# A new issue table for an attention and gated-MLP kernel on one Trainium2 core

## The chip, the cores and the metric

The kernel runs on one core of a Trainium2 chip. The metric is the device time of one launch in microseconds, as the median of several runs. Matrix products run on TensorE (PE in the profile, its weight loads PEld), elementwise work on VectorE (DVE), ScalarE (ACT) and GpSimd (POOL). SyncE (SP) issues the loads and stores.

## The reference

Two parts run one after the other: a recurrent linear attention over 768 steps for 4 batches and 8 heads of width 48, and a gated MLP on its output.

```python
for t in range(S):
    cur = einsum('bhd,bhe->bhde', u[None] * kt, vt)
    y[:, :, t] = einsum('bhd,bhde->bhe', rt, state + cur)
    state = wt[:, :, :, None] * state + einsum('bhd,bhe->bhde', kt, vt)
...
h = maximum(x @ w_in, 0.0)              # x: 4 x 768 x 384, w_in: 384 x 1024
u, v = h[..., :512], h[..., 512:]
v_n = (v - mean(v)) / sqrt(var(v) + 1e-06)
v_s = einsum('ts,bsd->btd', w_spatial, v_n) + b_spatial[None, :, None]
return (u * v_s) @ w_out
```

## The kernel before

**Attention.** Each batch is cut into 6 chunks of 128 steps, so there are 24 slots. A slot loads its decays W, keys and queries kr and values v (and, from slot 6 on, N, from which the bonus term is made on VectorE and POOL). slot_prep multiplies neighbouring decays (W2p, L442), scans them into F and E (L449, L454) and scales the keys and queries (L446, L456, L460). slot_a (L525), slot_d (L616), slot_y and slot_inter (both L560) are the small matrix products. They use the array in 64-wide pieces; everything else on TensorE uses it at full width. slot_x copies the output y, transposes it (yt, L669) and splits it into a high and a low part (xT).

**MLP.** Every product is made of three matmuls of split operands, high by high, high by low, low by high (mm3, L686 to L688). hv_unit makes the v half of the first layer (ph, 512 wide), scale normalises it (vh, vl), g_unit makes the u half (pu) and the spatial product (pv), adds the bias (L792), multiplies by us (L794) and splits the result into gh and gl (L796, L797). out_unit is the last layer (po) and its store (ot). In the first stretch the weights are loaded and split too (e_, wi, wo, ws, L350 to L361 and L329 to L331). check_w loads the decays once more (Nw) to check their range, in the buffer that N also uses.

**Buffers.** N has one buffer, W, v and dg two, kr three, the small accumulators in PSUM (ph, pu, pv, po, yt, pt, pg) three among them.

**The order of the work.** Each step is an op with the engines that it may run on and their costs in us, 1930 in all, 624 of them on TensorE. The string PLAN has one word for each op, in the order in which the code creates them: a letter for the engine (T TensorE, V VectorE, A ScalarE, G POOL, S SyncE) and a start in hundredths of a microsecond, in base 36. plan (L199) reads the table and sorts the ops by start; issue writes the instructions in that order. An engine takes its instructions in that order, and each waits for what it needs by semaphores, so a start is never a time that the chip keeps: it fixes the order on each engine, the fillers, and nothing else. fill puts filler matmuls (py<-zk, L893) into gaps that the table has on TensorE before the op `last`:

```python
for o, w in zip(self.ops, words):
    o.on, o.start = w[0], int(w[1:], 36) / 100
    assert o.on in o.eng
return sorted(self.ops, key=lambda o: o.start)
...
if t < last.start and o.start - b > GAP:
    cold = max(0.0, min(o.start, COLD) - b)
    warm(max(0.0, cold - 0.1) / 0.43 + max(0.0, o.start - max(b, COLD) - 0.1) / 0.224)
t = max(t, o.start + o.eng["T"])
```

Of the kernel before, what the change touches and what calls it, by code (L numbers as in the profile page):

```python
# [37 lines left out]
V504 A5k2 V5o3 S4it V4wy V4zd V51f V55w A5mc V5rn T27w T29t T2e2 A2hs A2jk A2mh S5k S7s Sgo Vur Tyf Vlw Vwp  # L38
V1ca Vov Vwg V137 V13w Gzk G1f3 A1un A1ty Gfo V1d8 T1ke V1p8 A1fo T12s A1ax T1ov T1vv T1fr V1j8 A1kc V22l T1ym
A20y V23b T26n A28i T2bq A2ct T2j2 T2lj T2o5 A2t0 A2w8 A2wv Smc Sbd S1es V18w T1lv G1dh V1ml V1jy V1fd G1i1  # L40
V1iv V1nj G1o1 V1ya A29k A2a9 V24n T256 V2da A24j T1r9 A1sr T2c7 T2fz T23t V288 A2dv V302 T2ho A2ju V2ll T2ng
A2pa T2qv A2ry T2ts T2vp T2xm A305 A35x A36k A3bf G3xh V3lw G3x1 G3y9 G3z1 G3zt V40i V41z A457 V4cq A41g A43s
V45n A4aq A4e4 G4im S1do S1fw S224 V28y T2rc G22t G2di V2an V25z V27z V2f3 V2jw G2k5 V2o1 A343 A3aq V2x1 T39s
V3cs A388 T31e A32w T2zj T3jt T382 V3c1 A3e5 V3l0 T3l7 A3py V3s9 T3ur A3w1 T3yq A40e T44m T473 T490 A4cp A4fj
A4jd S1pg S210 S2j9 V2vd T3b9 V2uf V30t V37e V2yd V35u V39n V3ac G39w G3ed A3ut A3hs V3n7 T3i1 V3tl A3ng T3h5
A3in T3vf T41u T3ml V3rj G3ss V3ve T438 A46m V484 T4cs A4ft T4k1 A4l4 T4mp T4pa T4r7 A4ud A4w5 A4wt S2g8 S2lb
S3mk V3hf T3nz G3cr V3j3 V3k2 V3em G3l8 V3mu V3oj G3n3 G3u3 A4a1 V41h V3wv T40d V49f V40q T3qz A3sh T4ax T4dh
T3z7 V47c V4bz T4f7 A4h7 V4io T4ly A4n8 T4ot A4pw T4t4 T4v1 T4wy A4zh A51a A51x A54q V585 V55o G57g V58o V597
G59w V5av V5e0 A5hl V5l3 A5ei A5pt V5tc V5bf A5d2 V5fa T5nq S3rn A47o S4aj A4qy S4tt A56b S596 A5r8 T32a T33q
# [999 lines left out]
```

## Time and profile before

| | |
|---|---|
| time, median of 3 runs | 366.39 us (364.48 to 369.11) |
| span of the profiled execution | 363.9 us; its time outside the span is not recorded |
| TensorE busy | 355.2 us, 98% of the span |
| VectorE busy | 277.7 us, 76% |
| ScalarE busy | 211.4 us, 58% |
| POOL busy | 138.2 us, 38% |
| DMA | 47.81 MB, mean 131 GB/s |

The page counts an engine as busy while an instruction of it runs. Matmuls are pipelined: one starts before the one before has ended, so a TensorE that is busy all the time can still be fed at more or less than its full pace. Times in the trace are from the first instruction; times in the table are from the table's own zero, and the two are compared at landmarks, operations that can be found in both.

### The profile page before, as it was taken

The numbers are of one execution on the slowest core, as the hardware profiler recorded it, in microseconds if no ns is written. First come the engines' busy times: TensorE is split into PE (matmuls) and PEld (weight loads), VectorE is DVE, ScalarE is ACT, GpSimd is POOL, SyncE is SP. The second block draws the span as 40 slices with busy tenths as digits, with TensorE's granted clock in tenths as the row PEclk, the third lists the DMA queues.
The fourth block names the chain that finished last, engine by engine and source line by source line (L and its number), as shares of the span: only waits on it lengthen the run. The fifth ranks groups of instructions, "written<-read, shape, count | busy, mean of one in ns | idle before, by whom it ended". The sixth has DMA issues, their size and how long they took to land.

```text
span 363.9 us, 11371 instructions
## 1 busy us (share of the span) xinstructions
PE 355.2 (98%) x4666; PEld 328.1 (90%) x4666; DVE 277.7 (76%) x591; ACT 211.4 (58%) x585; POOL 138.2 (38%) x182
## 2 busy tenths in 40 slices
PE   7999899999999999999999999999999999999998
PEld 6887686799999889799999999999999998899997
DVE  7899996888798988987999865878996876234330
ACT  2468896994555657792554587762454757721212
POOL 3334343412551665523641748133223514013220
PEclk9899999999999999999999999999999999999999
DMA  7977636564165365841456444613462441000101
GB/s 219 292 237 217 191 87 182 188 193 156 45 192 147 102 193 161 216 127 52 117 148 192 130 123 149 193 45 112 118 188 60 137 139 46 0 23 0 38 31 69
DMA packets 21546, 47.81 MB, mean 131 GB/s; under 512 B 2545, under 2 KB 10354, under 8 KB 21490
## 3 DMA queue, kind: packets, MB, share of 16 engines
q1 hardware_dynamic: 21346, 46.85, 43.8%
q8 instruction: 37, 0.61, 0.7%
q14 instruction: 19, 0.16, 0.2%
q10 hardware_dynamic: 144, 0.20, 0.1%
HBM read 42.32 MB, written 4.72 MB: 129 GB/s over the span
## 4 chain that ended last, share of the span: by engine, by line
PE 84%; DVE 7%; ACT 5%; issue 2%; DMA 1%; POOL 0%; DVEq 0%; ACTq 0%
PE pv L686 9%; PE pv L688 9%; PE pv L687 9%; PE py L560 6%; PE po L686 5%; PE po L688 4%; PE po L687 4%; PE ph L686 4%; PE ph L688 4%; PE ph L687 4%; PE pu L686 4%; PE py L893 4%; PE pu L688 4%; PE pu L687 3%; PE paw L525 3%; PE paw L616 3%
## 5 line engine op out<-in xcount | busy, mean ns | idle before, releaser
L686 PE MATMUL pv<-ws,vh 128*128 128x384 f32 x192 | 65.7, 342 | 0.2 <-ACT us L783 0.2
L688 PE MATMUL pv<-ws,vl 128*128 128x384 f32 x192 | 64.4, 335 | 0.0
L687 PE MATMUL pv<-ws,vh 128*128 128x384 f32 x192 | 64.3, 335 | 0.0
L792 DVE TENSOR_TENSOR t<-pv,b_sb 128x384 f32<-128x384 f32 x32 | 17.6, 552 | 26.8 <-PE pv L688 26.7
L686 PEld LDWEIGHTS pv<-ws,vh 128*128 128x128 f32 x192 | 36.0, 188 | 1.4 <-ACT us L783 0.9
L796 ACT CAST gh<-t 128x384 fp32r<-128x384 f32 x32 | 15.9, 512 | 36.5 <-DVE t L794 25.1
L687 PEld LDWEIGHTS pv<-ws,vh 128*128 128x128 f32 x192 | 36.1, 188 | 0.0
L688 PEld LDWEIGHTS pv<-ws,vl 128*128 128x128 f32 x192 | 36.0, 188 | 0.0
L686 PE MATMUL pu<-xT,wi 128*128 128x384 f32 x96 | 34.2, 357 | 0.0
L686 PE MATMUL po<-wo,gh 128*128 128x384 f32 x96 | 32.8, 342 | 0.0
L688 PE MATMUL pu<-xT,wi 128*128 128x384 f32 x96 | 32.4, 338 | 0.1
L688 PE MATMUL po<-wo,gl 128*128 128x384 f32 x96 | 32.3, 336 | 0.0
L687 PE MATMUL po<-wo,gh 128*128 128x384 f32 x96 | 32.3, 336 | 0.0
L687 PE MATMUL pu<-xT,wi 128*128 128x384 f32 x96 | 32.2, 336 | 0.0
L686 PE MATMUL ph<-wi,xT 128*128 128x512 f32 x72 | 30.6, 425 | 1.0 <-DVE bv L491 0.7
L688 PE MATMUL ph<-wi,xT 128*128 128x512 f32 x72 | 28.4, 394 | 0.0
L687 PE MATMUL ph<-wi,xT 128*128 128x512 f32 x72 | 28.2, 392 | 0.0
L505 ACT ACTIVATE AS<-id,dgs 128x64 f32<-128x64 f32 x76 | 20.1, 336 | 5.9 <-DVE dgs L497 5.8
L460 POOL TENSOR_TENSOR kr<-kr,E 112x512 f32<-112x512 f32 x13 | 16.4, 1264 | 15.8 <-DVE kr L446 7.6
L456 POOL TENSOR_TENSOR kr<-kr,F 112x496 f32<-112x496 f32 x13 | 16.2, 1247 | 15.2 <-DVE kr L446 6.7
L446 POOL TENSOR_TENSOR kr<-kr,W 112x256 f32<-112x256 f32 x16 | 16.1, 1009 | 15.0 <-DVE dgs L497 5.1
L794 POOL TENSOR_TENSOR t<-t,us 128x384 f32<-128x384 f32 x9 | 9.6, 1068 | 31.1 <-DVE t L792 29.5
(199 smaller groups left out, 969.7 us busy)
## 6 DMA issues: line engine op xcount, KB each, us to landing
kr<-in_tr_dram SPq DMA_DIRECT2D x24, 448.0 KB, 4.8
N<-in_nat_dram SPq DMA_DIRECT2D x18, 384.0 KB, 3.5
Nw<-in_gt_dram SPq DMA_DIRECT2D x16, 384.0 KB, 3.4
W<-in_tr_dram SPq DMA_DIRECT2D x24, 225.8 KB, 3.3
v<-in_nat_dram SPq DMA_DIRECT2D x24, 192.0 KB, 3.9
out_dram<-ot SPq DMA_DIRECT2D x18, 192.0 KB, 3.3
wst<-in_w_spT_dram SPq DMA_DIRECT2D x12, 192.0 KB, 3.7
out_dram<-ot SPq DMA_DIRECT2D x10, 96.0 KB, 3.6
```

What stands on the lines that cost most here:

```text
L446: op({"G": 0.9, "V": dve(half)}, lambda e, n=n: e.tensor_tensor(two(kr()[:, n])[:, :, :, n], two(kr()[:, n])[:, :, :, n], w_()[:, :, :, 1 ...
L456: op({"V": 0.68, "G": 1.07}, lambda e: e.tensor_tensor(seg(kr()[:, 0])[:, :, :L2 - 1], seg(kr()[:, 0])[:, :, :L2 - 1], F()[:, :, 1:].unsqu ...
L460: op({"V": 0.69, "G": 1.1}, lambda e: e.tensor_tensor(seg(kr()[:, 1]), seg(kr()[:, 1]), E().unsqueeze(3).broadcast_to([R, SUB * G, L2, 2]) ...
L505: e.mul(As()[:, j, g, :], id64, dgs()[:, j, g:g + 1])
L525: nc.tensor.matmul(pa()[ks, j, g * L:(g + 1) * L], kr()[rs, 0, ts_], kr()[rs, 1, ts_], start=True, stop=True)
L560: nc.tensor.matmul(py()[row][L * a:L * (a + 1), D * n:D * (n + 1)], x, z, start=(a, row) not in started, stop=not left[0], skip_group_chec ...
L686: nc.tensor.matmul(ps, ah, bh, start=first, stop=False)
L687: nc.tensor.matmul(ps, ah, bl, start=False, stop=False)
L688: nc.tensor.matmul(ps, al, bh, start=False, stop=last)
L792: op({"V": dve(HT)}, lambda: nc.vector.tensor_tensor(t1(), pv()[:, :HT], b_sb[:, tsl], ALU.add), r=[(pv, 0), ("b", 0)], w=[(t1, 0)])
L796: op({"A": act(HT)}, lambda: nc.scalar.copy(gh(), t1()), r=[(t1, 0)], w=[(gh, 0)])
L893: nc.tensor.matmul(pw, zk, zk, start=False, stop=True, skip_group_check=True)
```

## The change

The diff replaces the table, and nothing else. The number of words is the same. 292 words name another engine than before (instructions on VectorE: 578 words before, 583 after; ScalarE 404 and 394; POOL 169 and 174; TensorE 624 and SyncE 155 in both), the rest another start. The first word of the table stands for a filler matmul, the last three for the range check (L919 to L923). Cut to its first and last lines:

```diff
--- before.py
+++ after.py
 PLAN = """
-T2s S4g Tgq Aji Ajc S4x5 S5kl S6o Apg Vrs Vt1 Vxn Azp G12f Spf A1ph V1tz V1wl V1zy A221 G24f Sa0 A134 V15y
-V178 V1al A1co V1kw S28 S3c S8w Vib Tkh Vbe Vk0 Vky Vcx Gf4 Vfy Vgm Vmu Goq A115 A14p Vcc Vzc Ts1 V11e Toz Ar1
-T13o T15x Tx1 V10n A15e V1ej T18f A19v V1h2 T1s5 A1vc T1xl A23h Suq A1we V21n V2bl V2g0 A2qc G2xa Sng A1mu
-V1r1 V1sa V1uw A2gd V2i8 S1h0 A2kw V2n4 V2pq V2sq A2us V345 S2v6 A3to G496 S238 A3gn V439 S25r A34s V38c S3xz
-A4i8 V4r1 S4c7 A5nh V5qb S4ux A5gg V5ms S2sw A5tl G5yv S5jh A5uq V61n S1i4 A2o6 V2rf S5v7 A67e V6i0 S4jx A5af
-V5hp S4y9 A5l7 V6jc S1je A2yj V31r V32u V363 A3d0 V5co S2i5 A3ju V3m4 V3q7 V4h2 A53l V5j1 S2qm A3m6 V4gb V4pq
...
-Anl5 To7a To8q Toei Tofy Toom Toq2 Vos4 Goty Aoww Gp8c Tnll Tnpx Tnrd Anwe Tpnb Tpor Tpw0 Tpxg Tq1s Tq38 Vq5a
-Vq70 Aq8p Gqae Tnn1 Tnoh Tnst Anvc Tq4o Tq64 Tq7k Tq90 Tqag Tqbw Vqdy Vqfl Aqhb Vqiv Toxb Toyr Tp5z Ap81 Tpq8
-Tpro Tpt4 Tpuk Tpyw Tq0c Vq2e Gq48 Aq76 Vq8q Tqho Tqj5 Tqm1 Tqnh Aqpj Sqr3 Tqdc Tqes Tqox Tqqd Aqsf Sqtz Tqg8
-Tqkl Tqrt Tqt9 Aqvb Sqwv Vn8u Tnlb Vp1v
+T2j S3j Tay Ad7 Ade S3oy S2on S5l Amk Voj Vqe Vse Axq Vzt Snc A1k8 V1ma V1qh V1t3 A1v4 G1y7 S9p A138 V15h V16q V1ac
+A1gz V26o S2i S4k S8o Vh2 Tj4 Vax Vj2 Vk0 Vc6 Ve6 Veq Vfe Vky Vmm Ax2 Az7 V78 Vxk Tow Vu2 Tn2 Apq Tz9 T12f Tx1 V12s
+A14u V1c0 T17r A19n V1cr T1eg A1fx T1he A1ig S1ao A2ar V2ep V2iz V2lm A2q1 V2ta Sod A1q3 V1s6 V1us V23b A25c V2hb S25b
+A2ir V2kp V2na V2qo A2ve V2xs S3jg A40k G430 S15d A32n V3ol S4ch A4tr V4xq S2po A46i V4na S3yl A4uw V4wf S4gl A58z
+V5cd S4ej A50e V51w S4ox A5i9 G5lb S2f5 A45d V4bs S57i A5xp G627 S58j A5jz G64u S4y2 A5el G5nz S2d2 A388 V3ae V3ca
+V3ho A4bd V50c S2nm A3ar V4d3 V4ek V4g7 A4z9 V54h S2e3 V4b2 V4du V4hi V4l8 A52m V582 S47l V4ki V4mk V4z1 V55s A57t
...
+Soyy Tmfv Tmhb Tmir Amks To37 To4n To63 To7j To8z Toaf Vocg Voe2 Aofq Gohd Tmk7 Tmln Tmvs Amxs Toup Tow5 Toxl Tp4t
+Tp6a Tp7q Vp9q Vpdy Api1 Gpjv Tn30 Tn4g Toow Aoqx Tpc2 Tpdi Tpey Tpge Tphu Tpja Vplb Vpmy Apol Vpq3 Tnxe To0b To1r
+Ao3r Toz1 Tp0h Tp1x Tp3d Tp96 Tpam Vpcm Vpf9 Apgw Vpie Tpm7 Tprz Tptf Tpxr Apzs Sq17 Tpkq Tpnn Tpuv Tpwb Apyc Spzr
+Tpp3 Tpqj Tpz8 Tq0o Aq2o Sq43 Vm4p Tq24 Vq2z
 """
 
 GAP, FILL_TO, COLD = 0.3, 5, 7.0
```

Where the prediction gives a planned start, it is such a word: the first ph of the old table is `T27w`, 28.76 us, its first pv starts at 70.54 and its last po at 347.49 us; the new table's at 337.20 us, with the range check's matmul (L921, at 305.75 us in the old table) behind it at 337.72. The op `last`, up to which gaps get fillers, stands at 73.34 us in the old table and at 141.85 in the new one.

## Rows read from the trace of the kernel before

**Rows 1.** The page: span, and busy time of the engines.
```profile
span 363.9 us, 11371 instructions
...
PE 355.2 (98%) x4666; PEld 328.1 (90%) x4666; DVE 277.7 (76%) x591; ACT 211.4 (58%) x585; POOL 138.2 (38%) x182
```

**Rows 2.** Busy time by stretch: stretch, length, then PE, PEld, DVE, ACT, POOL, clock, DMA.
```profile
0.00:28.00 28.00, 24.99 (x346) 22.20 (x346) 24.26 (x53) 12.93 (x33) 9.90 (x23) 0.94 0.87 252
28.00:75.00 47.00, 43.59 (x703) 35.48 (x703) 40.49 (x86) 39.85 (x109) 19.93 (x24) 1.00 0.59 173
75.00:360.00 285.00, 284.37 (x3602) 268.32 (x3601) 212.99 (x454) 158.11 (x444) 108.32 (x135) 1.00 0.39 113
```

**Rows 3.** What TensorE waited for, 28 to 75 us, then 75 on: us, times, longest.
```profile
PE paw L616 <- DVE S L631: 0.8, 1, 0.8
PE ph L686 <- DVE bv L491: 0.7, 1, 0.7
...
PE ph L686 <- DVE t L792: 0.3, 1, 0.3
PE pv L686 <- ACT us L783: 0.2, 1, 0.2
```

**Rows 4.** Busy time by stretch, 30 to 90 us, columns as in rows 2.
```profile
30.00:50.00 20.00, 18.96 (x285) 15.13 (x279) 19.52 (x38) 17.99 (x55) 9.56 (x8) 1.00 0.59 168
50.00:70.00 20.00, 18.48 (x362) 14.76 (x353) 15.83 (x37) 15.67 (x39) 9.42 (x16) 1.00 0.56 168
70.00:90.00 20.00, 20.00 (x174) 19.32 (x173) 16.84 (x39) 15.66 (x40) 4.03 (x7) 1.00 0.62 186
```

**Rows 5.** Instructions of ph, pv, po: count, ns (least/median/most), first and last start.
```profile
L686 PE MATMUL ph<-wi,xT x72: 387/397/684, 31.0 to 314.6; 128*128 128x512 f32 x72
...
L686 PE MATMUL pv<-ws,vh x192: 333/334/446, 78.0 to 353.1; 128*128 128x384 f32 x192
...
L686 PE MATMUL po<-wo,gh x96: 332/336/444, 95.4 to 359.3; 128*128 128x384 f32 x96
```

**Rows 6.** The timeline of TensorE, full-width matmuls: start, us, instruction.
```profile
352.58 0.33 PE L686 MATMUL pv<-ws,vh 128*128 128x384 f32 x1
...
353.10 0.33 PE L686 MATMUL pv<-ws,vh 128*128 128x384 f32 x1
```

**Rows 7.** The chain in order of time, one run of small matmuls: start, us, work.
```profile
215.40 1.08 PE py L560 x64
216.47 0.48 PE paw L525 x32
216.96 0.43 PE paw L616 x14
```

**Rows 8.** What VectorE waited for, 28 to 75 us.
```profile
DVE bv L491 <- PE py L560: 3.2, 1, 3.2
```

**Rows 9.** Lines on VectorE and POOL, columns as in rows 5.
```profile
L446 DVE TENSOR_TENSOR kr<-kr,W x32: 400/418/1385, 7.2 to 274.9; 112x256 f32<-112x256 f32 x32
...
L456 POOL TENSOR_TENSOR kr<-kr,F x13: 1038/1227/1847, 12.7 to 286.3; 112x496 f32<-112x496 f32 x13
```

**Rows 10.** Loads of N and kr: us to landing; who waited for N.
```profile
  POOL N L467: 1.6, 1
  DVE N L467: 0.7, 2
DMA to landing us min/median/max: 2.8/3.5/5.2
...
kr<-in_tr_dram SPq DMA_DIRECT2D x24, 448.0 KB, 4.8
```

**Rows 11.** The end: last store (KB, us to landing), and the loads of `bad`.
```profile
out_dram<-ot ACTq DMA_DIRECT2D x1, 192.0 KB, 1.9
...
L990 SPq TENSOR_LOAD <-bad x1: 479/479/479, 336.6 to 336.6; - x1
L990 PEldq TENSOR_LOAD <-bad x1: 742/742/742, 360.1 to 360.1; - x1
```

More of the change, by code (lines that the diff above doesn't have):

```diff
@@ new lines @@
+V2zt T3a1 V3ec A35q T36a A39j T3in T3m0 T3bd V3dm A3ew V3m6 T3na A3qd V3t8 T3wo V3y5 T427 A44a T47p T4az T4cv A4fd
+A4h5 A4in S2c1 S27d S39f V38q T3cs G340 V3b5 V3jj V36e G3gl V3j7 V3kh G3dr V3mw A3le A3ko V3qu T3pa V3uj G3qz T3kb
+A3m3 T3xc T3zc T3oj V3sh G3w7 T40m V42u V44i T471 V48i T4ai A4ci T4es T4go T4il A4l3 A4mv A4ni A4pj G4sb V4r8 G4rw
+G4sy V4tl V4u3 V4un V537 A56f V59d A5a4 A5cg V5e8 V4v5 A4wr V5fx Tay1 S3fr A3uu S3xk A48q S4bg A4q2 S4ss A53r T2w5
+T2xl T34u A3c2 T54x T59a T5aq T5f2 T5je T5kv V5pm V5u7 A5vu V67s T2z1 T30h T31y A33y T50l T56e T57u T5gi T5nr T5p7
@@ new lines @@
+V5r7 V5x5 A65q V6gi T33e T3f3 T3gj A3ij T5qo T5s3 T5uz T60s T654 T66k V6as V6dw A6fj G6ja T42o T444 T45l A47o T521
+T53h T5c6 T5dm T5hy T5mb V5ob G5qn A66w V6ck T6jr T6l7 T6tw T6vc A6xc S99e T6ib T6mn T6xg T6yw A74s S85w T6o3 T6pj
+T6r0 T6sg A6ug S6vv T4kh T4lx T4ou A4sp T5tj T5wf T63o T68w T6ff T6gv V6j4 V6u8 A6yf G702 T4nd T4qa T4t6 A4y6 T7js
+T7o5 T7pl T7r1 T7sh T7xi V7zi G81b A870 V88i T4rq T4um T4z5 A51k T7gw T7ic T7l9 T7mp T7tx T7vd V82r G84j A88v G8aj
+T5xv T5zc T628 A64o T70d T71t T739 T74p T765 T77l V7cu V7ky A7mm V7uc T8c7 T8dn T8f3 T8io A8ko Sa0d T8aq T8h7 T8k4
@@ new lines @@
+T8lk V8sc S8ty T9rk T9t0 T9ug T9vw A9xx S9zc S346 S3ao S56h S3nx G3um V3pw G3s9 V3wf V42m V445 V45t G45n V4iu V5hm
+V5jv V5lh A5dw G48h V5qy A5n4 A5yu A5rh A5zg T4xh V63n T49m A4hg V5t9 T6ao T4we V573 A5fr V5si T6by A6go V6lq T6ws
+V749 T791 A7cd T851 T86y T88u A8bc A8d4 A8dr S3kt S3zm S5n3 S4fk V4qb V5ix V5zs V4rj V57v V65g V664 V5vi V693 V5yg
+V60q V62c A6e6 A5wz A6av V6c3 A6ew A6bh G6oa T6dr V72g A626 T680 A69n T7aq T6co V6ni A6zk V75j T7ef A7iv V7ma T7wt
+A7ya T84k A85y T8n0 T8xt T8zq A928 A967 A96u S4di S4z2 S63y S6ev G6ax G6ly V6ta V6o8 V6rw V6yl V70r V6q8 G74i V6f7
@@ new lines @@
+V6ht V6kg A6vi A75u V6t2 V6n2 V6na V78w A723 T7c0 V7f8 A7df T79i A7b5 T80m T7dc V7ib V7rl V7so T82y A84w V8d5 T8gj
+V8i0 V8r1 T8u0 T8vx T91m A944 A95w A98r A9as G9g6 V9ef G9fr G9gt G9hg V9i5 V9kb A9mu A9p6 G9r4 Aa0e Aa7y Ga9w V9ym
+Aa6i Vb9p S611 S6du S6m2 S7cn G72x V77y V6s4 V76a G7cz V7e5 V7j2 V79v V7pw V6vn V6xa V6yx A7nr A886 V70j A7fy V7kq
+G7g7 G7o0 T7za V8vb A7zd T7g0 A7hn T93v T81w V8a2 A8vk V91w T96g V98d V9ar T9pf V9qw V9si Ta70 Ta8x Taat Aadq Aafo
+Aagb S6ww S7gc S70k S82j G7mf V8eg V7te V7o8 V89u V8as V8bg G8fv V8p4 V7bi G7di V7h1 A8fo G8d6 A8lq V8x4 V92n A8mc
@@ new lines @@
+G93n T954 V9fl G98b T8sp A8uc T9mk T97q V99t G9b0 V9he T9nu A9qm V9tt Ta09 Aa5g Vaaa Tade Tafb Tah7 Aajp Aalh Aam4
+S7hd S84x S7in S95s G8l4 G8is G8mq V8tn V8xc V8xw V8yk V909 G958 V7wr G7yj V81g V9kj A9yz A8p2 V8qt V9aj A9ub V9en
+T9kh V9zw V9jk T995 A9bc Ta45 T9lt V9v4 V9w6 Ta5f Va7d Va8y Tacq Vaek Vag6 Taj4 Tal0 Tamx Aapf Aat0 Aatn Aavo Vawz
+Vax5 Vaxo Gayd Vaz0 Vazi Vb01 Ab5q Abbj Vbhn Vb5i Ab9u Gbbr Vb0k Ab25 Vbfz S83k A8ge S8j4 A8y2 S90s A9cj S9f9 A9ro
+T9a1 T9q4 Ta0x Aa9e Tbey Tbkq Tbm7 Tbp2 Tbqj Tbrz Vc2a Gc48 Ac9q Gcgo T9bh T9cx T9ed A9ls Tc8m Tcaq Tcc6 Tcf2 Tcgi
@@ new lines @@
+Tchz Vcjz Vcs6 Acw0 Vczx T9ft T9h9 T9ip A9kq Tbge Tbhu Tbja Tbxr Tbz7 Tc0n Vc42 Vc6y Ac8l Vd4y T9xc T9ys Ta2d Aa4e
+Tb6z Tb8f Tbnm Tbtf Tbuv Tbwb Vbyc Gce0 Acgw Vd18 Tdcz Tdef Tdfw Tdhc Adjc Sdkr Tdjg Tdkw Tdmc Tdns Vdpt Shj3 Td77
+Td8n Tda4 Tdbj Addq Sdls Tapp Tav4 Tawk Ab7p Tcdm Tcjf Tckv Tcmb Tcp7 Td3u Vd9m Gdcx Adgq Vdiw Tayb Tb17 Tb2n Ab4n
+Tdp9 Tdqp Tds5 Te09 Te5a Te6q Veeb Geg3 Aej9 Vere Tazr Tb43 Tb5j Ab8s Teeo Teg4 Tele Tesj Tetz Texc Vf3f Vf7x Aff3
+Vfi2 Tcnr Tcx5 Tcyl Ad0m Tdtl Tdv1 Tdxd Tdyt Te2e Te3u Ve5u Ved0 Afdo Gffc Tfm4 Tfnk Tfrw Tftc Afvd Si9y Tgy9 Th21
@@ new lines @@
+Th3h Th4x Ah8l Sha0 Tfp0 Tfqg Tg1a Tg3f Vg8e Sga1 S8k5 S98e S9ue S9oh G922 G9l6 V9im V93w G99l V9c3 V9cr V9oj Va1p
+Va40 Ga5s Vabk Aasb A9zp Aaff Aadg Aad7 Gag7 Aaxf Tarh Vb2k Taot Aar3 Tba7 Tast Vb1t Gb31 Vb4j Tbct Abg0 Vbjk Tca2
+Vcbi Vcd4 Td01 Td1y Td5a Ad7s Adaj Ades S9af S9vf Sad6 Sa62 V9nl Gada Vam2 V9wy Ga01 Va3d Vacv Gahr Vap9 Vany Vasm
+Vau9 Vall Vavk Vbjc Vbco Abb9 Gbk1 Abda Tbbh Vbuq Vbf7 Tau8 Aaw8 Tc3b Tbdj Vbl3 Abm6 Vbzv Tc4l Ac6j Vcgg Tdis Adke
+Vdnw Tehk Tejh Teqn Aet5 Aeux Aevk S9pi Sa7c Savv Sbgr Vakn Vaw1 Van0 Vaqy Vb59 Vbse Vbt2 Gblm Gbz6 Vb6r Vb8e Vbbe
@@ new lines @@
+Abvd Vc3l Abh2 Abd1 Vbkv Abho Vboi Tc5u Vcla Ac0x Tc23 Ac3q Tcrv Tc76 Vcfq Aci2 Vcn3 Tcuh Ad9h Vdz4 Te1p Ae36 Ve84
+Temu Teor Tevf Aexx Aezp Af0c Af2d Vfba Vf98 Vf9s Vfbs Gfcg Gfd3 Gfdq Afp2 Ag2y Gg59 Afg9 Afil Gfv3 Vgjf Agvj Vh05
+Sanc Sbep Sbd0 Sc7j Gbv7 Gbsk Gbws Vc0l Gc2r Vcnu Vcoi Gcjc Vcqi Vbpg Vbr3 Vbwk Vd4g Adq1 Ac4y Vbzn Vc5e Gcm6 Vd3i
+Tct5 Vdm3 Acti Tcqn Acsa Te8i Tcvq Vd69 Gdg4 Ve0f Te9s Vebp Vevg Tf5i Af6z Vf9z Tg4v Tg6r Tg8o Agb6 Agfk Agg7 Sbfq
+Sc6i Sby5 Sd1d Vcth Vcyz Vd70 Vd7y Gdfl Vdgc Vdh0 Gda3 Gdm9 Gc8e Gcbb Vcef Gelu Vdr4 Ackk Adau Aekf Vd2k Vemp Teb1
```

112 lines of the change are left out of this document (34 added, 78 removed).

## The prediction

> **What bounds the kernel now.** I read the page's busy line first: TensorE is busy for 98% of the span, VectorE for 76%, and no other engine above 58% [rows 1]. A busy TensorE can be one that waits between pipelined matmuls or runs fillers, so the second view is busy time by stretch: TensorE is idle for 3.0 of the first 28 us, 3.4 of the next 47, and 0.6 of the last 285 [rows 2]. The third view, TensorE's own waits, says the same: from 28 to 75 us it waited for VectorE's sums (S) and products (bv), from 75 on for two things of 0.3 and 0.2 us [rows 3]. So the kernel has two regimes. Up to about 75 us TensorE waits for what VectorE prepares, which is itself nearly full: 19.5 of 20 us from 30 to 50 [rows 4]. After that TensorE alone sets the pace and a new order has almost nothing to take away.
>
> The fourth view is the trace laid beside the table. The table's words are planned starts, so each landmark of TensorE has a planned and a measured time. The first ph was planned at 28.8 and started at 31.0; the first pv 70.5 and 78.0; the last po 347.5 and 359.3 [rows 5]. The kernel thus runs 2.2 us late at the first ph, 7.5 at the first pv, 11.8 at the end.
>
> **The change part by part.** Nothing is added or removed: 1930 words before and after, 624 of them for TensorE. 292 words name another engine (POOL gets 5 instructions more, VectorE 5 more, ScalarE 10 fewer), all get another start. By the diff the last po moves from 347.5 to 337.2, so at face value the table promises 10.3 us. I don't take that at face value, because the old table charges TensorE for things that the new one prices lower: 64-wide operations at 0.5 where the new steps are 0.39 to 0.48, and idle slots of 0.20 before full-width work.
>
> *One price list for both.* Three 384-wide matmuls step on in 0.52 us: 352.58 to 353.10 [rows 6]. A run of four small-array operations takes 1.08 + 0.48 + 0.43 = 1.99 us [rows 7]; I book 0.46, 0.45, 0.48 and 0.39 for its four parts and 0.12 for each change of array width. With ph at 0.69 (its step in both tables) and the tables' other costs this makes 322.1 us of work ahead of the last po in the old order and 322.4 in the new one, which changes width 66 times against 62. What a landmark's time exceeds the work before it is TensorE's lost time.
>
> *Up to the first ph (11.4 us of work).* Old table 28.8, trace 31.0, new table 23.8 for the same work: it lets the first three slots' attention run ahead of the weight preparation, and emits 33 filler matmuls instead of 38. The trace's lateness of 2.2 us at this point I keep: VectorE was busy for 24.3 of the 28 us in front of it [rows 2], so there is no cover that would shrink it. 23.8 + 2.2 = 26.0, a gain of 5.0. Ends: a lateness of 0 (7.2 us won) and one of 7.2 (nothing won); I stay at what the row shows.
>
> *From there to the first pv (39.7 us of work).* The trace took 78.0 - 31.0 = 47.0, so 7.3 were lost. After the first pv 10.4 were lost over 526 operations and 20 small-array runs with hardly a wait; this stage has 75 operations and 6 runs, so about 2 of its 7.3 are the same hand-over cost that any order pays. The other 5.3 are waits. One is plain: VectorE once sat 3.2 us for TensorE (bv), and TensorE then waited for bv [rows 3, 8]. The new table has TensorE gapless from 25.7 to 112.6, so by its own count none remain. It buys this by filling VectorE: the idle time that the table leaves VectorE between 30 and 90 us falls from 10.7 to 4.6 us (starts, less the code's cost, less the 0.08 by which successive instructions overlap). VectorE instructions stretch when POOL reads at the same time: L446 takes 0.42 typically and 1.39 at worst, POOL's L456 1.04 to 1.85 [rows 9]. The table prices all of them at the short end. I take S = 4.5 us of waits, a little under the 5.3 of the trace, since the 3.2 us wait hung on the old order while the stretching stays. Ends: 0 (table) and 11.4 (second rival).
>
> By the Trainium skill, "SBUF — State Buffer", section "Who interferes with whom", a VectorE instruction with two SBUF inputs and a GpSimd instruction that reads SBUF exclude each other, and the later one blocks for the whole of the earlier. That speaks against this change: the time that the tables book for this pair from 30 to 90 us is 67.7 of 60 in the new one and 61.8 in the old, so by the rule alone 5.9 us more than before have to give way, S = 5.3 + 5.9 = 11.2 and 369.2 us, the second rival by another road. The trace agrees in part: the worst L446 lost 0.97 us, but the median, 0.418 against a least of 0.400, shows no block in most [rows 9].
>
> *From the first pv to the last po.* Trace 359.3 - 78.0 = 281.3 for 270.9 us of work, 10.4 lost, spread thin. I keep 10.4. The new order has 271.3 us of work here, and one hole that the old one had not: TensorE idles 1.5 us at 112.6 until the keys of slot 10 are ready (filled with five filler matmuls). 271.3 + 10.4 + 1.5 = 283.2. Bounds for the hole: 0, if TensorE is late there anyway, to 3, if VectorE is later still.
>
> *SP's queue and the DMAs.* Every load is moved with its step. Up to 130 us the old table has 5 loads whose first user stands within 4.1 us of the issue, the new one 16, mostly N, Nw and v. N lands 2.8 to 5.2 us after its issue, median 3.5; kr 4.8 [rows 10]. Behind a late N stand VectorE's whole queue (the product L467 is next in line) and, on SP, the kr and v loads. I put 0 on it in the sum, as ends 0 and 3.2 (11 more loads at about 0.3), because TensorE's work in this stretch lies 1 to 4 us behind its inputs in the new table.
>
> *The tail.* In the trace 363.9 - 359.3 = 4.6 us follow the start of the last po [rows 1, 5]: the last copy, its store, which lands 1.9 us after its issue [rows 11], and the end of the program. The new table moves the range check to the very end: its one-column matmul and the one-element comparison that writes `bad` now follow the last po, and only then can the five engines load `bad` (0.48 us on SP, 0.74 on TensorE) and branch [rows 11]. These lie beside the last copy and the 1.9 us of its store, so I count 0, with 0 and 0.7, one such load, as ends.
>
> *Sum.* 26.0 + 39.7 + 2.0 + S + 283.2 = 350.9 + S for the last po, against 359.3: a gain of 8.4 - S, with S = 4.5 a gain of 3.9. The profiled span becomes 360.0. The profile records no time of its own execution outside the span; the runs' median of 366.4 lies 2.5 above the span, the fastest run 0.6. I carry the gain over to the median: 362.5 us.
>
> **Rivals.** *The waits vanish too.* S = 0.4: 366.4 - 8.0 = 358.4 us. For it: TensorE has no gap in the table, and hand-overs are booked as short as the trace has them. Against: the old table was nearly as gapless here (2.1 us) and the trace lost 7.3.
>
> *VectorE and POOL slip: slower than before.* Place: 30 to 90 us. The old table's 10.7 us of VectorE slack took part of the stretching; the new one has 6.1 less. If all of that comes through to TensorE, S = 5.3 + 6.1 = 11.4, a loss of 3.0: 369.4 us. It decides from S = 8.4 on. For it: VectorE was busy 52.2 of these 60 us already [rows 4]. Against: from 70 us on TensorE was not tied to VectorE at all, 20.0 of 20 busy.
>
> *Loads just in time.* The 11 tighter loads cost their 3.2: S = 7.7, 365.7 us, no change. For it: the single N buffer makes these loads a serial chain. Against: in the whole trace POOL waited 1.6 us for N and VectorE 0.7 [rows 10].
>
> *The table keeps its word.* 10.3 us: 356.1. Against it stands the price list above.
>
> **How the numbers follow.** Forecast, S between 2.5 and 6.5: 0.48 (360.5 to 364.5). Waits vanish: 0.22. Just-in-time loads: 0.13. Slip: 0.14. Table's word: 0.03. The range leaves out the table's word, the better part of the first rival and the worst third of the slip: 357.5 to 369.0. A measurement of this kernel tells about 2% from no change, 7.3 us. Faster by more: the table's word and, of the first rival, the part with S under 1.1, together 0.15. Slower by more needs S above 15.7, the end of the slip: 0.04. Within: 0.81.
>
> **What would show it.** Right: first ph near 25 us and 11.4 us of work done by 26; first pv (51.1 us of work) near 72; TensorE idle under 1 us after 115 apart from the hole; last po near 356. The waits between 30 and 90 should name VectorE, its busy time there above 54 of 60 us. Wrong: TensorE idle at 110 to 120 of several us (slip), VectorE waits on N or v of more than 1 us in sum (loads), or a last po under 353 (no waits). If TensorE loses much less than 10 us after the first pv, the hand-over cost was not fixed, and the step that kept it was wrong.

## The result, and the profile after

The changed kernel takes 362.92 us (360.93 to 364.02, 9 runs) where the kernel before, on the same chip, takes 366.32 (364.48 to 369.11, 9 runs): a ratio of 0.9899, interval 0.9866 to 0.9932. The forecast was 362.5. In a second series (the last experiment) the same two kernels gave 360.60 and 366.20, ratio 0.9867 (0.9839 to 0.9894). So the change is worth 1.0 to 1.3%, real and below the 2% bound. The kernel before has medians of 365.9 to 366.3 us in all five series of this study, so ratios of different series can be compared.

The total came out as forecast. Its parts did not, so the hit is in good part luck. The page after, for [rows 1]:

```profile
span 361.1 us, 11353 instructions
...
PE 356.2 (99%) x4656; PEld 331.1 (92%) x4656; DVE 271.3 (75%) x596; ACT 211.1 (58%) x587; POOL 141.1 (39%) x187
```

Busy time by stretch after, for [rows 2] and then [rows 4], columns as there:

```profile
0.00:28.00 28.00, 25.35 (x289) 23.13 (x290) 22.41 (x49) 11.39 (x30) 9.21 (x21) 0.89 0.81 222
28.00:75.00 47.00, 46.87 (x814) 39.48 (x815) 44.10 (x97) 42.72 (x117) 19.37 (x27) 0.99 0.72 211
75.00:361.00 286.00, 284.02 (x3556) 268.46 (x3554) 204.80 (x451) 156.98 (x442) 112.54 (x140) 1.00 0.37 111
...
30.00:50.00 20.00, 20.00 (x332) 16.29 (x326) 19.05 (x38) 17.64 (x53) 8.20 (x10) 1.00 0.71 216
50.00:70.00 20.00, 19.87 (x382) 17.06 (x383) 18.48 (x44) 18.68 (x48) 10.14 (x14) 1.00 0.79 224
70.00:90.00 20.00, 20.00 (x173) 19.68 (x173) 18.76 (x44) 16.43 (x46) 5.03 (x7) 1.00 0.50 151
```

From 28 to 75 us TensorE is idle for 0.13 us where it was idle for 3.4. VectorE is busier: it works for 56.3 of the 60 us from 30 to 90, where it worked for 52.2 before, and TensorE hardly waits for it there. All of TensorE's waits of 0.2 us or more between 28 us and the last po, for [rows 3] (the 0.5 us stand at 196.6, the 0.2 at 91.1):

```profile
PE yt L665 <- DVE y L661: 0.5, 1, 0.5
...
PE pt L539 <- ACT us L779: 0.2, 1, 0.2
```

ph, pv and po after, for [rows 5] (the lines stand four lower in the changed kernel, so L686 is L682):

```profile
L682 PE MATMUL pv<-ws,vh x192: 331/334/446, 75.3 to 350.3; 128*128 128x384 f32 x192
...
L682 PE MATMUL po<-wo,gh x96: 332/336/445, 95.4 to 356.5; 128*128 128x384 f32 x96
...
L682 PE MATMUL ph<-wi,xT x72: 386/390/505, 30.7 to 308.4; 128*128 128x512 f32 x72
```

The first ph starts at 30.7, hardly sooner than the 31.0 of before; the forecast had it near 25. With the prediction's price list the trace splits into its three stages and the tail (us). "Again" is a second profile of the same changed kernel, an experiment below.

| | before | forecast | after | again |
|---|---|---|---|---|
| to 11.4 us of work | 31.0 | 26.0 | 31.3 | 28.3 |
| from there to 51.1 | 46.9 | 46.2 | 43.1 | 43.0 |
| from there to the last po | 281.4 | 283.2 | 282.1 | 282.3 |
| last po to the end | 4.6 | 4.6 | 4.6 | 4.6 |
| span | 363.9 | 360.0 | 361.1 | 358.2 |

The first stage gained nothing instead of 5.0 us, the second 3.8 instead of 0.7, the third lost 0.7 instead of 1.8. Errors of +5.3, -3.1 and -1.1 us leave 1.1 of span: the first two cancel by chance.

**Where the first stage lost its 5 us.** TensorE's first steps after; columns are start, us, engine, line, operation. L889 is the fillers, L415 slot 0's bonus (pg0), L521 slot 0's slot_a (sc0), L612 its slot_d (pd0); further down sc1 is slot 1's slot_a, and KT0 and yt0 are slot 0's transposed keys and output:

```profile
6.70 2.50 PE L889 MATMUL py<-zk 128*128 128x128 f32 x10
8.99 1.71 PE L415 MATMUL pg<-up_sb,rk 112*128 112x2 f32 x8
...
12.46 1.13 PE L521 MATMUL paw<-kr 48*64 48x64 f32 x32
13.53 3.32 PE L889 MATMUL py<-zk 128*128 128x128 f32 x20
16.78 0.67 PE L612 MATMUL paw<-v,KT 64*64 64x48 f32 x32
```

Two things are to be seen. pg0's operand rk0 was ready at 7.6 us, but ten filler matmuls, issued for a gap of the table, ran until 9.2. pd0's accumulators were free at 14.4, when VectorE's copy of sc0 (L525) ended, but twenty filler matmuls held TensorE until 16.8; the table had pd0 at 11.9. And the eight bonus matmuls take 1.71 us, which is 213 ns from start to start; at 2.4 GHz it is 112. TensorE ran at 1.2 GHz up to 15.3 us and again from 22.1 to 28.9. The granted clock by stretch (the last three columns are clock, DMA share, GB/s; ahead of the trace's first clock entry the column shows 1.00 whatever it was, and only the pace of equal matmuls tells):

```profile
0.00:15.29 15.29, 12.95 (x96) 12.37 (x97) 11.66 (x28) 4.51 (x10) 2.81 (x15) 1.00 0.86 219
15.29:22.11 6.82, 6.52 (x116) 5.64 (x116) 6.47 (x12) 2.61 (x7) 3.69 (x4) 1.00 0.90 267
22.11:28.94 6.83, 6.83 (x85) 6.07 (x85) 5.15 (x13) 5.16 (x15) 3.15 (x3) 0.50 0.49 151
28.94:75.00 46.06, 45.93 (x810) 38.55 (x810) 43.23 (x96) 41.83 (x115) 18.93 (x26) 1.00 0.74 216
```

That gives the theory for the first stage, called theory 1 below, which the experiments test: TensorE itself is late, by fillers and by its clock, and VectorE waits for it. For the second stage there are two candidates, the new order and the 292 new letters.

### The profile page after: what moved, and what is told of

It is laid out like the page before. It is cut to its first block, busy times and chain, and to the rows that moved or that the text cites. A ratio compares the mean times of both kernels' runs of the same rounds, so it can differ in the third digit from the quotient of the medians.

```text
span 361.1 us, 11353 instructions
## 1 busy us (share of the span) xinstructions
PE 356.2 (99%) x4656; PEld 331.1 (92%) x4656; DVE 271.3 (75%) x596; ACT 211.1 (58%) x587; POOL 141.1 (39%) x187
## 4 chain that ended last, share of the span: by engine, by line
PE 92%; DVE 4%; ACT 3%; issue 1%; POOL 0%; DVEq 0%
PE pv L682 9%; PE pv L684 8%; PE pv L683 8%; PE py L556 7%; PE ph L682 5%; PE ph L684 5%; PE pu L682 5%; PE ph L683 5%; PE py L889 4%; PE pu L684 4%; PE po L682 4%; PE pu L683 4%; PE po L684 4%; PE po L683 4%; PE paw L521 4%; PE paw L612 3%
## 5 line engine op out<-in xcount | busy, mean ns | idle before, releaser
L682 PE MATMUL pv<-ws,vh 128*128 128x384 f32 x192 | 65.6, 342 | 0.0
L682 PEld LDWEIGHTS pv<-ws,vh 128*128 128x128 f32 x192 | 36.1, 188 | 0.5
L682 PE MATMUL pu<-xT,wi 128*128 128x384 f32 x96 | 34.0, 354 | 0.1
L682 PE MATMUL po<-wo,gh 128*128 128x384 f32 x96 | 33.2, 346 | 0.0
L793 POOL TENSOR_TENSOR gl<-t,gh 128x384 fp32r<-128x384 f32 x14 | 14.7, 1053 | 44.4 <-ACT gh L792 44.2
L637 ACT ACTIVATE S<-S,prod 112x48 f32<-112x48 f32 x100 | 25.2, 323 | 9.3 <-DVE S L627 7.2
L711 ACT ACTIVATE hv<-ph 128x512 f32<-128x512 f32 x24 | 14.3, 594 | 27.7 <-PE ph L684 27.5
L682 PE MATMUL ph<-wi,xT 128*128 128x512 f32 x72 | 29.4, 409 | 0.0
L684 PE MATMUL ph<-wi,xT 128*128 128x512 f32 x72 | 28.3, 393 | 0.0
L683 PE MATMUL ph<-wi,xT 128*128 128x512 f32 x72 | 28.3, 392 | 0.0
L754 POOL TENSOR_TENSOR vl<-hv,vh 128x512 fp32r<-128x512 f32 x14 | 18.1, 1300 | 25.2 <-ACT vh L752 24.9
L779 ACT ACTIVATE us<-pu 128x384 f32<-128x384 f32 x32 | 15.1, 486 | 14.7 <-PE pu L684 14.6
```

The source lines that it names most:

```text
L637: e.mul(S1[i % 2][a][:, g, :], S0[:, g, :], Wc[:, g:g + 1])
L682: nc.tensor.matmul(ps, ah, bh, start=first, stop=False)
L683: nc.tensor.matmul(ps, ah, bl, start=False, stop=False)
L684: nc.tensor.matmul(ps, al, bh, start=False, stop=last)
L754: lambda e, hv=hv, vh=vh, vl=vl: e.tensor_tensor(vl(), hv(), vh().bitcast(F32), ALU.subtract),
L779: op({"A": act(HT, True)}, lambda: nc.scalar.activation(us(), pu()[:, :HT], AF.Relu), r=[(pu, 0)], w=[(us, 0)])
```

## The experiments

### No fillers ahead of pd0

```diff
-                if t < last.start and o.start - b > GAP:
+                if t < last.start and o.start - b > GAP and not 11 < o.start < 12:
```

> The changed kernel without the ten filler matmuls (20 records, 13.53 to 16.85 us) that stand in front of slot 0's decay product pd0, which started at 16.8 us though its input KT0 was ready at 12.65. Theory 1 (TensorE itself makes the first 30 us late, by fillers sized for the table's gap): pd0 starts at 12.7 to 13.5, 11.4 us of work are done by about 28 (31.3 in the changed kernel), time 359.5 to 361. Rival VectorE (the forecast's reason: VectorE is full here, 22.4 of 28 us): 11.4 us of work still done near 31, time 362.9. Rival clock (fillers are what lifts the granted clock): more of the stretch at 1.2 GHz, 11.4 us of work later than 32, time 363.5 to 365.

366.07 us, ratio 0.9984 (0.9954 to 1.0014), twelve runs from 363.4 to 369.1. Theory 1 by itself fails. The rival on the clock is nearest: the trace is at 1.2 GHz up to 27.8 us, and 11.4 us of work are done at 31.7. pd0 starts at 14.5, not at 13: it waits not for KT0 but for VectorE's copy of sc0, 13.7 to 14.4, which frees its accumulators, and sc0 was late already. What that wins is gone by sc1, at the slow clock. The profiled run was the longest of the twelve, so its end says nothing about the median; but it shows a loss of another kind, TensorE idle without a wait, in the middle of a row of 32 small matmuls:

```profile
59.60 0.58 PE L521 MATMUL paw<-kr 48*64 48x64 f32 x25 [1.74 <-issue]
```

### No fillers at all in the first 100 us

```diff
-                if t < last.start and o.start - b > GAP:
+                if 100 < t < last.start and o.start - b > GAP:
```

> The changed kernel without any filler in the first 100 us. Theory 1: 11.4 us of work done by 27 to 29, time 359 to 361. Rival VectorE: near 31, time 362.9. Rival clock: TensorE stays at 1.2 GHz up to 25 us or longer, real work there takes about twice its time, 11.4 us of work later than 32.5, time 364 to 366.

361.03 us, ratio 0.9854 (0.9818 to 0.9890): 1.9 us under the changed kernel's first series, level with its second one (360.60), so at least nothing is lost. 11.4 us of work are done at 29.3, 2.0 sooner than in the trace after, although TensorE is at 1.2 GHz up to 25 us at least: the bonus matmuls of slots 0, 1 and 2, the last from 20 us on, are all 213 ns apart, and the transposes pt at 25.4 us 204, where those at 39.0 are 97 apart. (From 27.6 us on the small matmuls run at their later pace, so it was not slow for the whole of the first 30 us.) Slot 0's steps in that trace, beside those of the changed kernel above:

```profile
7.76 1.84 PE L415 MATMUL pg<-up_sb,rk 112*128 112x2 f32 x8 [3.25 <-DVE rk L410]
...
10.37 1.13 PE L521 MATMUL paw<-kr 48*64 48x64 f32 x32
12.71 1.09 PE L612 MATMUL paw<-v,KT 64*64 64x48 f32 x32 [1.20 <-ACT vs L476]
```

pg0 now waits for VectorE's rk, 0.9 us behind the table, and pd0 is 0.8 behind where it was 4.9. By the first ph the lateness is back at 5.5. TensorE is busy for 11.96 of the 12 us from 16 to 28, at the slow clock, so the clock is the likely cause; no run without fillers has the fast clock beside it. The forecast's reason, a VectorE without cover, isn't it: VectorE gets more done in the same time here, 23.9 us busy of 28 against 22.4.

### More fillers from 12 to 24 us

```diff
-                b = max(t, free)
+                b = max(t, free); 12 < o.start < 23.6 and warm(1)
```

> The changed kernel with one filler more (two matmul records, some 0.33 us) in front of each TensorE step with a table start between 12 and 23.6 us. Rival clock: the stretch of granted clock 0.5 from 22.1 to 28.9 us goes or gets shorter, 11.4 us of work done by 29 to 30, time 360.5 to 362. Theory 1 (fillers stand in front of real work): 11.4 us of work later by 1 to 4, that is 32.5 to 35, time 364 to 367. Rival VectorE: TensorE's idle time takes the fillers up, no change, 362.9.

363.92 us, ratio 0.9973 (0.9935 to 1.0011), in two groups: seven runs from 363.1 to 364.1, five from 367.7 to 368.4. The profiled run, 367.7, has the granted clock down from 23.8 to 30.6 all the same and 11.4 us of work done at 36.3, 5.0 later. In that run fillers ahead of work cost more than theory 1's 1 to 4 us; what the faster group did is not in a trace.

### A long first gap, then almost none

```diff
-                    cold = max(0.0, min(o.start, COLD) - b)
-                    warm(max(0.0, cold - 0.1) / 0.43 + max(0.0, o.start - max(b, COLD) - 0.1) / 0.224)
+                    n = {394: 11, 1189: 3, 11401: 5}
+                    warm(n.get(round(100 * o.start), 0))
```

> The changed kernel with its early fillers laid out anew: 11 instead of 6 in the first gap (as many as the old table has there), 3 in front of pd0, none elsewhere in the first 100 us. Without any filler the first 30 us ran wholly at 1.2 GHz (eight bonus matmuls 213 ns apart, 112 at 2.4 GHz) and still 11.4 us of work were done 2 us sooner than in the changed kernel. Theory 1 (fillers in front of ready work cost, and the clock costs as well): the long first gap brings 2.4 GHz by 8 to 10 us at little cost, as in the run with the old head, 11.4 us of work done by 26.5 to 28, time 357.5 to 359.5. Rival: the later start of the spread matmuls (7 us instead of 3.4) delays everything behind it by as much as the clock gives, 11.4 us of work by 29.5 to 30, time 361. Rival: the clock falls again between 10 and 25 us, since TensorE idles there, 11.4 us of work by 29 or later, time 360.5 to 362.

365.98 us, ratio 0.9974 (0.9940 to 1.0008), 363.2 to 370.8. The last rival holds, and worse than stated: the clock is up at 5.7 us and falls at 9.1, at 19.3 and once more at 53.4. The second stage takes some 49 us, over 5 more than in the changed kernel: the second fall lasts into it, to 33.0, and the third lies in its middle. The stretches around it, and what TensorE did just before:

```profile
32.96:53.44 20.48, 19.39 (x340) 16.43 (x338) 18.53 (x39) 18.20 (x54) 8.43 (x9) 1.00 0.70 218
53.44:60.27 6.83, 6.83 (x46) 5.69 (x49) 5.30 (x14) 3.54 (x11) 3.65 (x6) 0.50 0.50 164
```

```profile
52.77 0.32 PE L612 MATMUL paw<-v,KT 64*64 64x48 f32 x7 [1.09 <-issue]
```

TensorE stood 1.09 us without a wait that the profile names, just ahead of the fall. In the changed kernel, 45.93 of 46.06 us busy after 28.9, the clock does not fall. But the stop alone is not shown to be the cause: the longer one without the ten fillers, 1.74 us at 57.9, was followed by no fall.

### The old head with the new rest

The 123 steps with an old start below 27.00 us keep their old word; all others take the new letter and the new start plus 4.00 us (two of them, which would come sooner, are put right behind the head). The first words:

```diff
-T2j S3j Tay Ad7 Ade S3oy S2on S5l Amk Voj
+T2s S4g Tgq Aji Ajc S402 S2zr S6o Apg Vrs
```

> The old table's first 123 steps (starts below 27.0 us, old letters, old order), then all the others in the new table's order and letters. The changed kernel's stage up to 11.4 us of work gained nothing, the one from there to 51.1 us of work took 43.1 us instead of 46.9. Theory 1: the gain belongs to the new order of that second stage and needs no new head: 11.4 us of work by 31, 51.1 by 74 to 75, time 362 to 363.5. Rival: the second stage runs well only because the new head has VectorE's work for slots 1 and 2 done sooner: 51.1 us of work at 76.5 or later, time 365 to 367.

364.46 us, ratio 0.9975 (0.9949 to 1.0001). In the trace theory 1 is right: 11.4 us of work at 30.5, 51.1 at 73.2, so the second stage takes 42.7 us with the old head too, and the last po starts at 354.9, 1.6 sooner than in the changed kernel. But the span ends 6.8 us later than that, not 4.6. The instructions of the last branch (ns, then the start):

```profile
L987 POOLq COMPARE_BRANCH  x1: 65/65/65, 356.6 to 356.6; - x1
...
L987 PEldq COMPARE_BRANCH  x1: 3767/3767/3767, 356.8 to 356.8; - x1
```

TensorE's own takes 3.77 us (0.39 in the changed kernel). In the last 5 us of this trace the DMA queue that loads instructions brings two blocks, of 16 KB each, where the changed kernel's brings one (queue, packets, MB, share). One of the two is under way from 357.9 to 359.3 us, inside that branch; the other, like the changed kernel's, comes behind it:

```profile
q8 instruction: 2, 0.03, 3.4%
```

### The same, TensorE's program 24 instructions shorter

```diff
-SPLIT, PE_END = 5, 10
+SPLIT, PE_END = 5, 4
```

> The kernel with the old head and the new rest again, with 4 instead of 10 filler matmuls behind the last step, so that TensorE's program is 24 instructions shorter (12 weight loads, 12 matmuls). With 10, TensorE's last branch took 3.77 us where it takes 0.4 in the other traces, and the span ended 6.8 us after the last po instead of 4.6. Theory (the long branch hangs on where the program's end lies, nothing else): the branch takes 0.4 us, time 364.46 - 2.2 = 362.3. Rival (it belongs to the old head or to the order): the branch stays at 3.8, time 364.5.

362.07 us, ratio 0.9882 (0.9855 to 0.9909), and TensorE's branch:

```profile
L987 PEldq COMPARE_BRANCH  x1: 393/393/393, 357.0 to 357.0; - x1
```

The long branch goes, one block is loaded, and the median falls by 2.4 us, for six fillers that follow the last step. So over 2 us hung on the length of TensorE's program. With that out of the way the old head with the new rest is as fast as the changed kernel within the intervals: the new head gains nothing that shows there, and the gain is the second stage's. What the new head is worth when the clock goes up early stays open: the last po starts at 355.2 here, at 356.5 in the first profile of the changed kernel and at 353.6 in the second one below.

### The new order with the old letters

> The changed kernel's order with the old table's engine letters (292 steps go back to their old engine). Theory (the gain from 11.4 to 51.1 us of work is the order's: loads and VectorE's work for later slots come sooner): 51.1 us of work done by 74 to 75.5, time 362.5 to 364. Rival (it is the letters': POOL and ScalarE take what VectorE had too much of): 51.1 us of work at 77 to 79, TensorE idle for 3 us or more from 28 to 75, time 365.5 to 368.

375.87 us, ratio 1.0261 (1.0220 to 1.0303). The rival holds for the second stage (46.2 us, against 43.1 with the new letters and 46.9 in the kernel before), and then the third takes 293.6. TensorE's longest waits from 28 us on:

```profile
PE pt L539 <- DVE t L788: 1.6, 1, 1.6
PE pv L682 <- DVE t L788: 1.4, 1, 1.4
PE ph L682 <- DVE xT L677: 1.3, 2, 0.8
PE ph L682 <- ACT xT L675: 1.1, 1, 1.1
```

### The old order with the new letters

> The old table's starts, and so the kernel before's order, with the new table's engine letters (the 292 steps on their new engine). The new order with the old letters took 375.9 us, 13 more than the changed kernel. Theory (starts and letters fit only together, since each order has VectorE, ScalarE and POOL just full where the letters were drawn for it): TensorE waits in several places after 50 us, time above 370. Rival (the new letters are better by themselves, and the order costs or gives nothing): 51.1 us of work done by 75, time 362 to 364.

379.60 us, ratio 1.0365 (1.0327 to 1.0404): the theory. The second stage takes 49.1 us, the third 291.5. Order and letters are one thing; either half alone is 10 to 14 us slower than the kernel before.

### The old order without fillers

The edit of the second experiment, in the kernel before.

> The kernel before without any filler in the first 73 us. Removing all early fillers made the changed kernel faster by 1.9 us although it then ran 28 us at 1.2 GHz. Theory 1 (there the fillers stood in front of work that was ready; in the old order VectorE, 11.7 of 12 us busy from 16 to 28, sets the pace and the fillers fill waits): the old order without fillers gains nothing and loses the clock, 11.4 us of work later than 31.5, time 367 to 370. Rival (fillers cost in any order): 11.4 us of work done by 29, time 364 to 365.

369.95 us, ratio 1.0089 (1.0061 to 1.0116): theory 1. 11.4 us of work are done at 33.8 (31.0), and up to 36.9 the clock is up only from 19.9 to 23.3. The same edit costs 4 us in the old order and nothing in the new one. Busy time from 16 to 28 us in the kernel before suggests why, columns as in [rows 2]:

```profile
16.00:28.00 12.00, 11.44 (x202) 9.59 (x201) 11.72 (x25) 7.39 (x22) 3.95 (x5) 1.00 0.84 268
```

VectorE is full there, 11.7 of 12 us (10.0 in the changed kernel), so TensorE would wait for it anyway, and the fillers can stand in those waits. This is argued from the row; no run moved the fillers of the old order.

### The new head with the old rest

All steps with a new start below 65.00 us keep their new word; the others take the old letter and the old start minus 6.32 us (14 of them, which would come sooner, are put right behind the head).

> The changed kernel's first 425 steps (starts below 65.0 us, new letters, new order), then all the others in the old table's order and letters, the range check at its old, earlier place. Theory (all of the gain is won before 75 us; after it TensorE alone sets the pace in either order): 51.1 us of work done by 74 to 75, from there to the last po within 1.5 us of the changed kernel's 281.8, time 361.5 to 364. Rival (the new order also saves something after 75 us, or the buffers left by the new head don't suit the old order): 366 or more.

368.70 us, ratio 1.0099 (1.0062 to 1.0135): the rival's 366 or more. TensorE has one long wait, at the seam:

```profile
PE pv L682 <- ACT vh L752: 4.1, 1, 4.1
```

Nothing like it is in the kernels before and after, so it is the splice's, as the rival's second half had it (what the new head leaves does not suit the old order), and the total does not tell whether the new order saves anything later on. The stage behind the seam does: from 60 us of work to the last po this trace takes 272.5 us in the old order, the changed kernel 272.8 in the new, the kernel before 271.9. After the second stage the new table is worth nothing: the three lie within 1 us. And 11.4 us of work are done at 28.3 here, 3.0 sooner than in the changed kernel, with the same steps and fillers; the clock was up from 6.1 to 19.7 us, not from 15.3.

### Fillers laid anew

```diff
-                if t < last.start and o.start - b > GAP:
+                if t < last.start:
...
+                    n = {394: 11, 1189: 6, 1269: 2, 1575: 1, 1682: 4, 1816: 1, 2027: 1, 2104: 2, 11401: 5}
+                    warm(n.get(round(100 * o.start), 0))
```

> The changed kernel with as many fillers (33), laid where TensorE waited in the runs without fillers or with a long first gap: 11 in front of the spread matmuls, 6 in front of pd0, 2 py0, 1 slot 0's state product, 4 pg2, 1 yt0, 1 sc1, 2 pt2, and the 5 of the later hole. Theory (held at 2.4 GHz from about 8 us and with no filler ahead of ready work, the first stage is as fast as VectorE lets it be): granted clock 1.0 from 10 us on, 11.4 us of work done by 27 to 28.5, time 358 to 360. Rival (the clock falls all the same between 9 and 33 us, as with the long first gap alone, 366.0): 11.4 us of work at 29.5 or later, time 362 to 366.

360.40 us, ratio 0.9865 (0.9831 to 0.9899). 11.4 us of work at 28.3, within the theory's 27 to 28.5, and a time 0.4 us above its range; but the clock was not held, which the theory wanted: it is up from 8.4 us, down from 11.8 to 15.2, then up for good. The lowest median of the study, but the interval overlaps those of no fillers (0.9854) and of the changed kernel, so it isn't shown to beat it.

### The changed kernel again

> The changed kernel once more, unchanged, for a second profile of its first 30 us. In the first one the granted clock went up at 15.3 us, fell from 22.1 to 28.9, and 11.4 us of work were done at 31.3; the run with the new head and the old rest has the same first 425 steps and the same early fillers, and there the clock was up from 6.1 to 19.7 us and the same work done 2.9 us sooner. Theory (the point at which the clock goes up differs from execution to execution, and the first stage with it): another point than 15.3; up by 6 to 10 us goes with 11.4 us of work done by 28 to 29.5 and a time of 360 to 361.5, up later with 30.5 to 32 and 362 to 364. Rival (the program alone sets it): up at 15.3 again, 31.3 within 0.3, time 363.

360.60 us, ratio 0.9867 (0.9839 to 0.9894). The clock is up from 5.6 us and falls once, from 19.2 to 22.7 (columns as above):

```profile
5.58:19.24 13.66, 12.69 (x200) 11.27 (x200) 13.40 (x28) 5.61 (x15) 4.62 (x5) 1.00 1.03 283
19.24:22.65 3.41, 3.41 (x43) 2.88 (x43) 2.90 (x9) 2.35 (x7) 2.33 (x2) 0.50 1.08 231
```

The same steps as in the first profile after:

```profile
6.28 1.38 PE L889 MATMUL py<-zk 128*128 128x128 f32 x10
7.76 1.02 PE L415 MATMUL pg<-up_sb,rk 112*128 112x2 f32 x8
...
9.81 0.69 PE L521 MATMUL paw<-kr 48*64 48x64 f32 x32
10.44 2.50 PE L889 MATMUL py<-zk 128*128 128x128 f32 x20
12.87 0.67 PE L612 MATMUL paw<-v,KT 64*64 64x48 f32 x32
```

The same twenty fillers now cost pd0 0.5 us (VectorE's copy ends at 12.4) instead of 2.4. 11.4 us of work at 28.3: the theory, and a profiled execution of 360.0 us. So the first stage's time is a draw: the same code takes 31.3 or 28.3 us, and the earlier clock goes with the shorter time in both profiles and in the run with the new head. The six times of this series fall into two groups as well, four from 360.0 to 360.7 us and two of 362.4 and 363.0; only one of them has a trace.

## Why the prediction was right, and where it was not

**Up to the first ph: the step failed.** "The trace's lateness of 2.2 us at this point I keep: VectorE was busy for 24.3 of the 28 us in front of it [rows 2], so there is no cover that would shrink it." The lateness was 7.5, not 2.2, and VectorE didn't make it: it was busy for 22.4 of 28 and waited for TensorE. What the forecast had not priced is that a filler is real work on the bound engine, sized by the table's gaps and, from 7 us on, for 2.4 GHz; when TensorE is late or slow, the filler delays it further. [rows 2] hid this behind a TensorE "busy" for 25.0 of 28 us. The runs bracket it: without fillers and at 1.2 GHz the lateness at the first ph is 5.5, with the clock up early and fillers 4.5. So 3.0 of the 7.5 go with the clock and with fillers at its slow pace. No run came below 4.5, so the 2.2 that the forecast kept was not reached in any way that was tried; what the rest is made of is read from one trace. The 4.5 of the second profile are 1.0 up to pd0, 0.5 up to yt0, where VectorE is late behind a collision with POOL, 1.3 up to sc1 with the clock down, and 1.7 up to the first ph, 1.1 of them a stop without a wait at 26.2. The end that the prediction gave this step, a lateness of 7.2, is close to what the first profile shows.

**From there to the first pv: right about VectorE, wrong about the wait.** The step is "I take S = 4.5 us of waits", with "the stretching stays". The stage took 43.1 us, so by the same sum S = 43.1 - 39.7 - 2.0 = 1.4. It took 42.7 to 43.2 in eight traces with the new order and letters there, whatever the head did; the two others (no fillers ahead of pd0, and the long first gap) had a stop without a wait in it, and one of them a fall of the clock. VectorE's stretching did stay: its product of the keys (L446 before) took 0.42 us on average from 30 to 90 us, and 0.51 after (L442; busy us and mean ns stand behind the first bar):

```profile
L446 DVE TENSOR_TENSOR kr<-kr,W 112x256 f32<-112x256 f32 x8 | 3.2, 419 | 0.1
```

```profile
L442 DVE TENSOR_TENSOR kr<-kr,W 112x256 f32<-112x256 f32 x7 | 3.6, 508 | 0.0
```

It no longer reached TensorE. So the step that failed is the one from VectorE's fill to waits of TensorE; what was found in its place is 0.13 us of idle time from 28 to 75 us. A full VectorE can be ahead of TensorE or behind it, and here order and letters together decide which: either half alone has this stage at 46.2 or 49.1 us. Which of their steps does it, no run shows. "The waits vanish too" had this stage nearly right, and its 358.4 is too low mainly because of the first one.

**From the first pv to the last po: right.** 282.1 against 283.2, and the hole at 112.6 costs 0.7 (98 to 100 us of work takes 3.2 us, before 2.5), not 1.5. The range check at the very end costs nothing, as the tail of 4.6 shows. The old order behind the new head, with its own letters, confirms that the two tables leave TensorE alone to count here. It is not so for any table: with order and letters mixed this stage takes 291.5 and 293.6 us.

**Loads: right at 0.** VectorE waited 0.5 us for N after (0.7 before), POOL 2.7 (1.6), and none of TensorE's waits hangs on it.

**The rival on VectorE and POOL: wrong in size, right in kind.** TensorE's row of waits has nothing of it after 28 us. It is there in single instructions. Slot 1's product on VectorE and POOL's beside it, in the changed kernel:

```profile
16.26 1.27 DVE L442 TENSOR_TENSOR kr<-kr,W 112x256 f32<-112x256 f32 x1
```

```profile
15.83 1.42 POOL L452 TENSOR_TENSOR kr<-kr,F 112x496 f32<-112x496 f32 x1 [0.54 <-DVE kr L442]
```

POOL's ends at 17.25 and VectorE's 0.28 later; it takes 1.27 us instead of its usual 0.42. (The second of the two long ones, 1.07 us at 35.9, also ends 0.28 us after POOL's.) The Trainium skill, "SBUF — State Buffer", section "Who interferes with whom", has the later of the two blocked for the whole of the earlier. These two lines agree. As a price for every overlap it would mislead: 11 of this line's 35 instructions on VectorE ran beside a working POOL instruction, and 2 of them took over 0.55 us.

**The signals.** VectorE above 54 of 60 us (56.3), TensorE idle under 1 us after 115 and the last po near 356 (356.5) came true. The first ph near 25, 11.4 us of work by 26 and the first pv near 72 (75.3) did not, and they point at the step that was wrong. The waits from 30 to 90 us that "should name VectorE" are not there: 0.13 us in all. One end of the range does not follow from the prediction's own sum: 357.5 us asks for S = -0.5, below the 0 that it gave as S's end.

## What to carry to other kernels

Take a forecast's total apart at landmarks before believing it: here two wrong terms cancelled. A filler matmul that keeps the clock up is work on the bound engine; check in the trace whether the next real step was ready while it ran, and take another profile before reading a difference in the first 30 us, since two profiles of the same code were 3 us apart there. An issue table is one object: its order with other engine letters, or its letters with another order, was 10 to 14 us slower than the kernel that both came from.

## What the runs showed of the hardware

**The point at which TensorE's clock goes up differs between executions of the same code**: 15.3 us in the first profile of the changed kernel, 5.6 in the second, 6.1 in a kernel with the same first 425 steps. The Trainium skill, "TensorE: Matmul & The Clock Gate", Part 1, says that the number of slow matmuls at the start varies from run to run and that the ramp is worth under 1% of a typical span. The two profiles agree with the first, and with the second as far as their difference goes: 3.0 us at 11.4 us of work, 0.8% of 361. That is also nearly the whole of the 3.4 us that this change was worth in the first series.

**TensorE's instructions are loaded in blocks while it runs, and a block can come late.** In the changed kernel one DMA queue brings 37 blocks of 16 KB, spread from 17.8 us to the end, while TensorE issues 9312 instructions; with 24 TensorE instructions fewer, the old head's 38 blocks became 37. TensorE stood for 1.1 to 2.2 us without a wait in the middle of rows of small matmuls, in five traces; in the second profile of the changed kernel here:

```profile
25.66 0.52 PE L556 MATMUL py<-S,kr 48*64 48x48 f32 x21
...
27.28 0.43 PE L556 MATMUL py<-S,kr 48*64 48x48 f32 x11 [1.10 <-issue]
```

A block was under way from 24.7 to 26.0 us, and TensorE went on 1.3 us after it had landed. The same holds for all five stops of over 1 us: 1.74 us without the ten fillers, 1.09 with the long first gap, 2.15 in the old order with the new letters and 2.05 at 25.3 us in the new head with the old rest ended 1.2 to 1.4 us behind a block's landing. So did the long branch of the old head (landing at 359.3, end at 360.6). For that branch the cause is shown, by the six fillers whose removal took 3.4 us from it; for the stops inside the rows the coincidence, five times out of five, speaks for the same cause, but no run removed one.
